# One attention-plus-MLP decode step on one core: the second and third pair's keys in one load each, their gathers moved to ScalarE and GpSimd

## The chip, the core and the metric

The kernel runs on one core of one Trainium2 chip. A core has five engines with an instruction queue each: PE (TensorE, matmuls), DVE (VectorE), ACT (ScalarE), POOL (GpSimd) and SP (SyncE, which here only issues DMAs). Sixteen DMA engines move data between HBM and the on-chip memory (SBUF). The metric is the device time of one execution in microseconds. Before the change its median over three runs is 189.87 us (189.81 to 189.93).

## What is computed

One new token (a row of 512 numbers) goes through grouped-query attention over a cache of 16384 positions and then through a small MLP:

```
q = layernorm(x) @ wq                          # 32 query heads of 128, 8 key/value heads
p = softmax(q . k_cache / sqrt(128))           # four query heads share one key head
h = x + (p . v_cache) @ wo
out = h + B(layernorm(h))                      # B: layernorm, w1 and w2 (one position: what they give is shifted
                                               #    out and padded with zeros), then gelu(layernorm(.) @ w3) @ w4
```

The caches have 8 heads of 16384 x 128 bf16 each, 4 MiB a head: 32 MiB of keys and 32 MiB of values. With wq, wo, w3 and w4 the core reads 79.17 MB in one execution, and each byte is used once. Position shifts in B leave nothing of w1 and w2 for a sequence of one position, so the kernel does not read them.

## The kernel before

**Pairs and halves.** The eight key heads are taken as four pairs. A pair's keys are 8 MiB: 128 partitions with 64 KB each (256 positions of 128 numbers). Its values have the same form. `kb_all` holds one pair's keys, seen as two halves `kb[0]` and `kb[1]` of 32 KB a partition; `vb` holds one pair's values; `kt` (32 KB a partition) holds half a pair's keys transposed. The first 4 MiB to arrive in `vb` are wq, and at the end wo goes into `kb[0]`, w3 and w4 into `kb[1]`.

**One pair** (the loop over `j` at the end of the function) goes like this:

1. DVE copies the pair's queries into `qn` (L704). For each half `y`, DVE transposes the keys from `kb[y]` to `kt` in 32x32 blocks of 4-byte elements (L616). A half has eight pieces. In pairs 0 to 2 an instruction takes two pieces, in the last pair mostly one.
2. PE clears a score bank (L627) and, piece by piece, multiplies queries and keys: four matmuls a piece, 32 a half (L633). DVE's transposes of the second half overwrite `kt` piece by piece as PE finishes the first half's.
3. `softmax` (L643 to L659): DVE's maximum, a small matmul that spreads it, ACT's exponential, and DVE's transposes of the result into `pt`. PE meanwhile runs 14 passes of two "unread" products (L498): matmuls whose result nobody reads, set in by `P.spin(14)` ahead of the matmul that sums the softmax (L678).
4. `values` (L670): 64 matmuls of `pt` with `vb` into the bank `O`.
5. `gather` (L687 to L696): DVE adds the four 128-column blocks of `O` with a mask weight each into `od` (one instruction, then three that continue it), PE multiplies `od` with `zo` (L694), and DVE scales the result into the pair's 32 rows of `o_m`. All on DVE and PE, so the next pair's `qn` copy and transposes stand behind it in DVE's queue.

**Who waits for what.** `Program` records every operation with what it reads and writes, and sets semaphore waits from that. Each engine runs its list in order. PE's part of the four pairs is not written out four times: `_tensor` emits one pair as a loop whose waits compare DVE's semaphore with a register that grows from piece to piece and from pair to pair. A wait for landed values goes through POOL: a no-op there waits for the DMA and then signals PE.

**Loads.** All large loads stand in SP's list and so in one order: wq, keys 0, values 0, keys 1 (two halves), values 1, keys 2 (two halves), values 2, keys 3 (two halves), values 3, wo (two parts), w3, w4 (three parts). Keys 0 are one load of 64 KB rows (L463 is the line of all loads, as a helper issues them). Half `y` of the next pair's keys is issued when DVE has transposed half `y` of this pair's; the next values when PE has read this pair's. An issued load stands behind the unfinished ones in the same queue.

**The end.** After the last pair DVE sums `o_m` (L732) and casts it (L734), PE runs 6 passes of unread products and multiplies with wo (L739), then follow layernorm (L743 to L531, ACT's L753), w3 (L759), gelu (L769), w4 (L782 and L794) and the 1 KB result's store.

Of the kernel before, what the change touches and what calls it, by code (L numbers as in the profile page):

```python
# [7 lines left out]
BF16 = mybir.dt.bfloat16  # L8
# [16 lines left out]
class Program:  # L25
# [150 lines left out]
    def _tensor(self):  # L176
# [51 lines left out]
        for o in loop:  # L228
            ds = [d for d in o.deps if d.own]
            assert not ds or o.at[0] == "value"  # L230
            assert not any(d.dma for d in o.deps)
            for d in ds:
                told.setdefault(o.at[1:3], set()).add((d.sem, d.val - d.worth + 1, d.val))
# [4 lines left out]
        assert v0 > 0 and first - step * last > 0  # L238

        r, rl, ry, rq, rk = (eng.alloc_register(n) for n in ("seen", "landed", "half", "query", "piece"))  # L240
        self.turn, self.turned = rk, KP * pieces
# [68 lines left out]
        def straight(kind):  # L310
            nonlocal now
            for a in places(kind, 1):
                self._spin(eng, at[a])
                v = rest.get((kind, a[-1]))
                if v is not None:
                    eng.reg_add(r, r, v - now)
                    eng.wait_ge(vector, r)
                    now = v
                self._issue(eng, at[a])
# [30 lines left out]
DH = 128  # L350
# [14 lines left out]
KP = 8 * DH  # L365
# [5 lines left out]
def bass_sequential_preLN__gqa_block_cached__mixer_s_mlp__decode_kernel(  # L371
# [13 lines left out]
    with ExitStack() as ctx:  # L385
# [60 lines left out]
        kb_all = sb("kb", [128, 256 * DH], BF16)  # L446
# [21 lines left out]
        def load_keys(j, y):  # L468
            n = 128 * DH
            load(f"k{y}", kb[y][:, :], pair_rows(A_k_cache, j)[:, y * n:(y + 1) * n], ("r", y, 0),  # L470
                 also=[("r", y, i) for i in range(1, RPARTS)])
# [55 lines left out]
        def variance(i):  # L527
# [7 lines left out]
            for n in range(1 + i):  # L535
# [9 lines left out]
        load("k", kb_all[:, :], pair_rows(A_k_cache, 0), ("r", 0, 0),  # L545
             also=[("r", y, i) for y in range(2) for i in range(RPARTS) if y or i])
# [65 lines left out]
        def transpose_keys(y, cuts):  # L612
            for t, n in zip(cuts, [b - a for a, b in zip(cuts, [*cuts[1:], 8])]):
                view = lambda x, t=t, n=n: x[:, :].bitcast(I32).rearrange("p (x l w) -> p x (l w)", x=2, l=64)[
                    :, :, t * 512:(t + n) * 512]
                P.op("DVE", lambda e, view=view: e.transpose(view(kt), view(kb[y])),  # L616
                     r=[("r", y, i) for i in range(RPARTS)], w=[("kt", t + i) for i in range(n)], worth=n)

        def key_piece(at, n):
            part = kt[:, :].rearrange("p (x f) -> p x f", x=2)[:, :, bass.ds(at, KP)]  # L620
            return part.rearrange("p x (l b s e) -> p b e x l s", l=8, b=2, s=32, e=2)[:, n // 2, n % 2, :, :, :]
# [40 lines left out]
        def values(j):  # L662
            tiles = vb[:, :].rearrange("p (x c l d) -> p x l c d", x=4, c=8, l=8)
            for x in range(VP):
                P.part("value", j, x)
                for it in range(16 // VP):
                    for ct in range(4):
# [4 lines left out]
                            tiles[:, l // 8, l % 8, 4 * ch:4 * ch + 4, :], start=(l < 2), stop=(l >= 30)),  # L672
# [8 lines left out]
        def gather(j):  # L681

            O, key = O_ps[0], ("O", 0)
            for c in range(4):
# [151 lines left out]
```

## Time and profile before

| | |
|---|---|
| median of three runs | 189.87 us |
| the profiled execution's own time | 189.89 us |
| its span, first to last instruction | 188.4 us |
| time outside the span | 1.49 us |
| busy: PE, DVE, ACT, POOL | 73%, 61%, 5%, 3% of the span |
| bytes read from HBM | 79.17 MB |
| mean granted TensorE clock | 0.898 of full |

The prediction reads four views. The page gives sums and the DMA engines' load. The timeline gives, for runs of like instructions, start, duration and in square brackets how long the engine had stood idle before and what ended that. The view of groups by shape gives the mean duration of one instruction of a kind. The view of windows cuts the span into stretches and gives PE's busy time, the granted TensorE clock (PEclk, 1.00 is full, 0.50 half), the share of DMA engines busy and the bandwidth in each; a transfer counts there with all its bytes where it starts, so in short windows the share can pass 1.

### The profile page before, as it was taken

Reading aid. Unit: us, or ns where it says so; the run is one execution under the profiler, and the core shown is the slowest. Engines: PE = TensorE matmul, PEld = TensorE weight load, DVE = VectorE, ACT = ScalarE, POOL = GpSimd, SP = SyncE. Lnnn points to the kernel's source line nnn. Section 1 sums busy time; section 2 is a strip of 40 time slices with the busy share of each in tenths; the row PEclk is TensorE's granted clock in tenths of the full one; section 3 lists DMA queues with packets and bytes.
Section 4 is the critical chain, followed back from the end, with each engine's and each line's share of the span. In section 5 each row is a group of like instructions: output and inputs, shape, how many; then the busy total and the mean of one; then the engine's idle time right before and its main releaser. Section 6 shows DMA issues by size and latency. Waiting matters only on the chain.

```text
span 188.4 us, 2532 instructions
## 1 busy us (share of the span) xinstructions
PE 137.8 (73%) x820; PEld 59.3 (31%) x824; DVE 115.8 (61%) x141; ACT 9.3 (5%) x16; POOL 5.9 (3%) x11
## 2 busy tenths in 40 slices
PE   1009700599989639998990999999319999886874
PEld 1004200234434413443450344345103433432332
DVE  4900741999645299994508999551449897513154
ACT  3000000000020000000200000020000000500011
POOL 1900000000000000000000000000000000000010
PEclk9999985569999975999998599999955999999998
DMA  6999999999799998999999999997999998899994
GB/s 223 445 445 445 445 445 445 445 445 445 334 445 445 445 543 362 417 389 403 445 445 445 445 445 445 445 445 334 445 445 445 556 403 362 362 440 450 397 411 183
DMA packets 2605, 79.19 MB, mean 420 GB/s; under 512 B 298, under 2 KB 300, under 8 KB 812
## 3 DMA queue, kind: packets, MB, share of 16 engines
q1 hardware_dynamic: 2596, 79.17, 97.9%
q8 instruction: 1, 0.02, 0.0%
q10 hardware_dynamic: 8, 0.00, 0.0%
HBM read 79.17 MB, written 0.00 MB: 420 GB/s over the span
## 4 chain that ended last, share of the span: by engine, by line
DMA 45%; PE 36%; DVE 16%; issue 2%; ACT 0%; SPq 0%; DVEq 0%
DMA kb<-in_A_k_cache_dram 32%; PE banks L633 22%; DMA kb<-in_B_w_dram 13%; DVE kt L616 12%; PE banks L498 6%; PE banks L670 4%; DVE mx L643 1%; PE banks L627 1%; DVE od L690 1%; PE banks L647 1%; PE banks L759 1%; PE banks L694 0%; DVE od L687 0%; DVE osum L785 0%; PE banks L782 0%
## 5 line engine op out<-in xcount | busy, mean ns | idle before, releaser
L616 DVE STREAM_TRANSPOSE kt<-kb 128x2048 int32<-128x2048 int32 (+1 forms) x37 | 71.0, 1985 | 10.4 <-DMA kb<-in_A_k_cache_dram 10.4
L633 PE MATMUL banks<-kt,qn 128*128 x256 | 69.1, 426 | 0.1
L633 PEld LDWEIGHTS banks<-kt,qn 128*128 x256 | 26.8, 105 | 41.0 <-issue 21.5
L498 PE MATMUL banks<-xn 128*128 128x512 bf16 x126 | 28.6, 381 | 0.0
L627 PE MATMUL banks<-qn 128*128 128x512 bf16 x8 | 3.9, 490 | 23.9 <-DVE kt L616 23.9
L498 PEld LDWEIGHTS banks<-xn 128*128 128x128 bf16 x130 | 12.7, 99 | 15.8 <-issue 2.4
L593 PE MATMUL banks<-vb,xn 128*128 x32 | 8.5, 432 | 9.7 <-DVE xn L584 9.7
L670 PE MATMUL banks<-vb,pt 128*32 128x512 bf16 x256 | 14.7, 379 | 0.7 <-POOLq L475 0.7
L659 DVE STREAM_TRANSPOSE pt<-p_sb 64x1024 bf16<-64x1024 bf16 x8 | 9.9, 1239 | 5.4 <-ACT p_sb L655 5.3
L655 ACT ACTIVATE p_sb<-banks,bias 128x1024 bf16<-128x1024 f32 x4 | 4.5, 1114 | 155.4 <-DVE nmh L651 155.4
L670 PEld LDWEIGHTS banks<-vb,pt 128*32 128x32 bf16 x256 | 8.7, 97 | 4.7 <-POOLq L475 0.8
L687 DVE TENSOR_SCALAR od<-banks,rowc 128x128 f32<-128x128 f32 x4 | 1.4, 351 | 14.2 <-PE banks L670 14.2
L643 DVE TENSOR_REDUCE mx<-banks 128x1 f32<-128x1024 f32 x4 | 4.9, 1224 | 8.1 <-PE banks L633 8.1
L627 PEld LDWEIGHTS banks<-qn 128*128 128x128 bf16 x8 | 0.8, 100 | 25.8 <-issue 25.4
L600 DVE STREAM_TRANSPOSE qcol<-banks 64x1024 f32<-64x1024 f32 x4 | 4.8, 1226 | 6.6 <-PE banks L593 6.6
L593 PEld LDWEIGHTS banks<-vb,xn 128*128 128x128 bf16 x32 | 3.5, 108 | 14.3 <-issue 11.6
L539 POOL TENSOR_TENSOR st<-st,expo 128x1 f32<-128x1 f32 (+1 forms) x2 | 1.3, 630 | 175.4 <-DVE st L537 175.4
L506 PE MATMUL banks<-mean 128*128 128x512 f32 (+1 forms) x12 | 6.5, 622 | 0.0
L694 PE MATMUL banks<-od,zo 128*32 128x128 f32 x8 | 1.6, 285 | 6.5 <-DVE od L690 6.5
L680 DVE RECIPROCAL den<-banks 32x1 f32<-32x1 f32 x4 | 0.6, 155 | 7.8 <-PE banks L678 7.8
L690 DVE SCALAR_TENSOR_TENSOR od<-banks,rowc,od 128x128 f32<-128x128 f32 x12 | 4.2, 351 | 0.4
L647 PE MATMUL banks<-mxd,mean 128*128 128x128 f32 x8 | 2.0, 326 | 2.4 <-DVE mxd L644 2.4
(81 smaller groups left out, 49.5 us busy)
## 6 DMA issues: line engine op xcount, KB each, us to landing
kb<-in_A_k_cache_dram SPq DMA_DIRECT2D x6, 4096.0 KB, 24.9
vb<-in_A_wq_dram SPq DMA_DIRECT2D x1, 4096.0 KB, 12.3
kb<-in_A_wo_dram SPq DMA_DIRECT2D x1, 3584.0 KB, 28.5
kb<-in_B_w_dram SPq DMA_DIRECT2D x1, 1792.0 KB, 24.2
kb<-in_B_w_dram SPq DMA_DIRECT2D x1, 896.0 KB, 26.0
kb<-in_B_w_dram SPq DMA_DIRECT2D x1, 640.0 KB, 27.1
kb<-in_A_wo_dram SPq DMA_DIRECT2D x1, 512.0 KB, 29.4
kb<-in_B_w_dram SPq DMA_DIRECT2D x1, 256.0 KB, 27.2
```

The source lines that it names most:

```text
L498: P.unread = lambda e: e.matmul(banks[:, 7, :], copies(xn[:, 0:1], 128), copies(xn[:, 0:1], 512), start=True, stop=True)
L506: pe(lambda e: e.matmul(banks[:, 7, 0:n], mean4[:, :], copies(mean4[:, 0:1], n), start=True, stop=True), r=["mean4"], w=["spare1"])
L593: pe(lambda e, k=k: e.matmul(row[:, bass.ds(P.b, 512)], copies(xn[:, k:k + 1], 128), wq_k[:, k, bass.ds(P.c, REP * DH)], start=(k == 0), s ...
L600: dve(lambda e, g=g, b=b, half=half: e.transpose(qcol[64 * g:64 * g + 64, 2 * b:2 * b + 2, :, :].rearrange("p e m u -> p (e m u)"), half.r ...
L616: P.op("DVE", lambda e, view=view: e.transpose(view(kt), view(kb[y])), r=[("r", y, i) for i in range(RPARTS)], w=[("kt", t + i) for i in r ...
L627: pe(lambda e: e.matmul(row[:, bass.ds(P.y, 512)], copies(none, 128), copies(none, 512), start=True, stop=False, skip_group_check=True), r ...
L633: pe(lambda e, n=n: e.matmul(row[:, bass.ds(P.y, 512)], qn[:, n, bass.ds(P.q, 128)], key_piece(P.k, n), start=False, stop=(n == 3), skip_g ...
L643: dve(lambda e: e.tensor_reduce(mx[:, :], s_all, AX.X, ALU.max), r=[("s", 0), ("s", 1)], w=["mx"], **both)
L655: act(lambda e: e.activation(p_sb[:, :], s_all, ACTF.Exp, bias=bias[:, 0:1], scale=float(SCALE), accum_out=acc[:, :]), r=[("s", 0), ("s", ...
L659: dve(lambda e, g=g: e.transpose(pt[64 * g:64 * g + 64, :, :, g, :], p_sb[64 * g:64 * g + 64, :]), r=["p"], w=["pt"])
L670: pe(lambda e, l=l, ct=ct, ch=ch: e.matmul(O_ps[0][32 * ct:32 * ct + 32, :], pt[:, l, ch, :, :].rearrange("p g u -> p (g u)"), tiles[:, l ...
L690: dve(lambda e, block=block, c=c: e.scalar_tensor_tensor(od[:, :], block, rowc[:, c:c + 1], od[:, :], ALU.mult, ALU.add), r=[key, "rowc", ...
```

## The change

- **Keys of pairs 1 and 2 in one load each.** They become one load of 64 KB rows, as keys 0 are already. Keys 3 stay two halves, because wo and w3/w4 are placed by halves after them. Instead of being issued in halves, such a load is issued when the transposes of *both* halves of the pair before are done, with one exception, the next point.
- **8 KB of shift a pair.** `kb_all` grows by 16 KB a partition. Keys 0 lie 16 KB into it, keys 1 8 KB, keys 2 and 3 at its start. So the next pair's keys do not overwrite the last 8 KB of this pair's, which are the last two pieces of the second half: the load does not wait for their transposes (the key `("tail", j)`).
- **Pieces.** A piece is now 16 neighbouring positions of a partition in one run (`KP` doubles) instead of 8 positions from each of two places; the sizes of all instructions stay. The second half is transposed piece by piece, eight instructions, in every pair. The indexing of `values` follows.
- **Three gathers on ScalarE and GpSimd.** In pairs 0 to 2 ACT scales the four blocks of `O` into `osum` (four activations), POOL adds them in two steps into `od`, PE waits for POOL; the result is scaled by ACT and masked by POOL into `o_m`. The last pair keeps the DVE form, and a no-op on POOL stands between DVE's `od` and PE.
- **Unread products growing by pair.** The passes ahead of L678 become a loop whose count is derived from the register of DVE's semaphore: 5, 8, 11 and 14 passes for pairs 0 to 3 in place of 14 each.

The core of the diff:

```diff
+                passes, body = self.spins.get(id(at[a]), (0, 0))
+                if passes:
+                    by = step // 3
+                    eng.reg_mov(self.turn, now - by * passes)
+                    eng.br("pe_turn")
+                    nc.switch_bb("pe_turn", parent=None)
+                    for _ in range(body):
+                        self.unread(eng)
+                    eng.reg_add(self.turn, self.turn, by)
+                    eng.br_lt(self.turn, r, "pe_turn", "pe_turned")
...
+                if any(d.own == "g" for d in at[a].deps):
+                    eng.wait_ge(self.gathered, rl)
...
-KP = 8 * DH
+KP = 16 * DH
+BASE = (4 * KP, 2 * KP, 0, 0)
...
-        kb_all = sb("kb", [128, 256 * DH], BF16)
+        kb_all = sb("kb", [128, BASE[0] + 256 * DH], BF16)
...
+            if y is None:
+                load("k", kb_all[:, BASE[j]:BASE[j] + 2 * n], pair_rows(A_k_cache, j), ("r", 0, 0),
+                     also=[("r", y, i) for y in range(2) for i in range(RPARTS) if y or i] + [("tail", j)])
...
+                at = BASE[j] + (8 * y + t) * KP
+                apart = BASE[j] and y and t >= 6
+                P.op("DVE", lambda e, t=t, n=n, at=at: e.transpose(
+                    kt[:, t * KP:(t + n) * KP].bitcast(I32), kb_all[:, at:at + n * KP].bitcast(I32)),
+                     r=[("tail", j)] if apart else [("r", y, i) for i in range(RPARTS)],
+                     w=[("kt", t + i) for i in range(n)], worth=n)
...
+            if j < PAIRS - 1:
+                for c in range(4):
+                    act(lambda e, c=c: e.activation(osum[:, c * 128:(c + 1) * 128], O[:, c * 128:(c + 1) * 128],
+                                                    ACTF.Identity, scale=rowc[:, c:c + 1]),
+                        r=[key, "rowc"], w=[("osum", c)], bank=[key])
+                pool(lambda e: e.tensor_tensor(osum[:, 0:256], osum[:, 0:256], osum[:, 256:512], ALU.add),
+                     r=[("osum", c) for c in range(4)] + [("o_m", j - 1)], w=[("osum", 0), ("osum", 1)])
+                P.op("POOL", lambda e: e.tensor_tensor(od[:, :], osum[:, 0:128], osum[:, 128:256], ALU.add),
+                     r=[("osum", 0), ("osum", 1)], w=["od", "gathered"], own="g")
+            else:
...
+                P.op("POOL", lambda e: e.nop(), r=["od"], w=["gathered"], own="g")
...
-                transpose_keys(y, (0, 2, 4, 6) if j < PAIRS - 1 else range(8) if y else (0, 1, 2, 4, 6))
+                transpose_keys(j, y, range(8) if y else (0, 2, 4, 6) if j < PAIRS - 1 else (0, 1, 2, 4, 6))
                 scores(j, y)
-                if j < PAIRS - 1:
+                if j == PAIRS - 2:
                     load_keys(j + 1, y)
+                elif j < PAIRS - 2 and y:
+                    load_keys(j + 1)
```

79 lines of the change are left out of this document (45 added, 34 removed).

## The prediction

> **What bounds the kernel now.** I read the page first: it says how full the DMA engines are.
>
> ```profile
> span 188.4 us, 2532 instructions
> ...
> PE 137.8 (73%) x820; PEld 59.3 (31%) x824; DVE 115.8 (61%) x141; ACT 9.3 (5%) x16; POOL 5.9 (3%) x11
> ...
> DMA  6999999999799998999999999997999998899994
> ...
> q1 hardware_dynamic: 2596, 79.17, 97.9%
> HBM read 79.17 MB, written 0.00 MB: 420 GB/s over the span
> ```
>
> SP's queue (q1) keeps the sixteen engines at 97.9% of the span. The DMA row gives their busy tenths in 40 slices: the first and the last slice are low, hardly any between. PE at 73% and DVE at 61% are the next busiest. That alone could hide small gaps, so I then took from the timeline the instructions that started because a load had landed.
>
> ```profile
> 13.14 0.29 DVE L584 TENSOR_SCALAR xn<-hT,st 128x4 bf16<-128x4 f32 x1 [3.54 <-DMA vb<-in_A_wq_dram]
> ...
> 32.47 17.66 DVE L616 STREAM_TRANSPOSE kt<-kb 128x2048 int32<-128x2048 int32 x8 [6.46 <-DMA kb<-in_A_k_cache_dram]
> ...
> 139.04 8.95 DVE L616 STREAM_TRANSPOSE kt<-kb 128x1024 int32<-128x1024 int32 x5 [3.17 <-DMA kb<-in_A_k_cache_dram]
> ...
> 148.74 9.13 DVE L616 STREAM_TRANSPOSE kt<-kb 128x1024 int32<-128x1024 int32 x8 [0.75 <-DMA kb<-in_A_k_cache_dram]
> ...
> 168.16 3.64 PE L670 MATMUL banks<-vb,pt 128*32 128x512 bf16 x64 [0.67 <-POOLq L475]
> ...
> 176.71 1.91 PE L739 MATMUL banks<-kb,o_b 128*32 128x512 bf16 x32 [0.17 <-DMA kb<-in_A_wo_dram]
> ...
> 182.29 0.94 PE L759 MATMUL banks<-kb,hc 128*32 128x448 bf16 x16 [0.34 <-DMA kb<-in_B_w_dram]
> ```
>
> These are the landings, in the queue's order, of wq, keys 0, the two halves of keys 3, values 3 (through POOL's no-op), wo and w3. Keys 0 (8 MiB) took 32.47 - 13.14 = 19.33 us. From there to the first half of keys 3 lie 44 MiB (values 0 to 2, keys 1 and 2, half of keys 3): 106.57 us, or 19.38 us for each 8 MiB. The next 4 MiB took 9.70 us (19.40 for 8), values 3 then 19.42. **One pace, 19.33 to 19.42 us for 8 MiB, from the second load to the last cache load:** the queue never ran dry, and no compute instruction between 13 and 168 us sets the end. After w3's landing a fixed chain of 6.1 us leads to the span's end (188.4 - 182.29).
>
> How far ahead of the queue is SP?
>
> ```profile
> 41.44 9.05 SPq L463 DMA_DIRECT2D kb<-in_A_k_cache_dram  x2
> 64.38 0.33 SPq L463 DMA_DIRECT2D vb<-in_A_v_cache_dram  x1
> 75.78 9.10 SPq L463 DMA_DIRECT2D kb<-in_A_k_cache_dram  x2
> ...
> 133.21 0.33 SPq L463 DMA_DIRECT2D vb<-in_A_v_cache_dram  x1
> ...
> 157.94 1.81 SPq L463 DMA_DIRECT2D kb<-in_B_w_dram  x4
> ```
>
> At 19.38 us a load, values 0 land at 32.47 + 19.38 = 51.85, keys 1 at 71.2, values 1 at 90.6, keys 2 at 110.0, values 2 at 129.3. Keys 1 were issued 10.4 us before values 0 landed (41.44), values 1 6.8 us before keys 1 landed (64.38), keys 2 14.8 us ahead (75.78), values 3 15.5 us ahead of the second half of keys 3 (133.21), w3 18.8 us before values 3 and wo were both in. So the kernel is bound by its bytes, and an edit can only count in four ways: the price of a load in the queue, a load issued too late, the chain before w3, the chain after it.
>
> **The change, part by part.**
>
> *Loads.* Two loads fewer, same bytes, same order. Two 4 MiB loads cost 2 x 9.70 = 19.40 us; whole 8 MiB loads cost 19.33 to 19.42. A merged pair thus gives -0.07 to +0.02 us, two of them -0.14 to +0.04. I take the middle, **-0.05 us**.
>
> The Trainium skill, page "DMA: Bandwidth & Descriptors", section "Anatomy of one DMA — SWDGE (gpsimd) path", speaks strongly for such a merge: it fits a DMA's time as about 2.0 us plus bytes at 436 GB/s. By that rule two loads fewer would save about 4.0 us (an estimate from that page). The trace does not agree for loads that stand behind others: 2.0 us more for each half would make 11.6 us, and the measured half took 9.70.
>
> *When the merged loads are issued.* This is what could cost something. In pair 0 the transposes start at 32.47 as before. The four instructions of the first half are done at 41.44, when SP issues. The second half is now eight instructions, as in the last pair: 9.13 / 8 = 1.14 us each. The load of keys 1 needs the first six: 41.44 + 6 x 1.14 = **48.3**. How long does an issue need until bytes flow?
>
> ```profile
> 0.74 0.40 SPq L463 DMA_DIRECT2D vb<-in_A_wq_dram  x1
> ```
> ```profile
> 1.60:1.80 0.20, 0.00 (x0) 0.00 (x0) 0.00 (x0) 0.20 (x1) 0.20 (x2) 1.00 2.06 494
> ```
>
> On the idle queue at the start: 1.60 - 0.74, about 1 us (the window row's last columns are DMA share and GB/s; the window before it moved nothing). From above: wq landed 12.40 us after its issue, where 4 MiB at the pace take 9.69, so at most 2.7 us with every start-up loss. Keys 1 must flow when values 0 end at 51.85: the issue may come between 49.1 (by 2.7) and 50.8 (by 1.0). At 48.3 it is in time by 0.8 to 2.5 us; I take the nearer row, 1.0 us, and so no gap. Keys 1 then land at 71.2 in one piece, and pair 1's transposes can only start there, as pair 0's did at their landing, while now the first half is at hand when DVE leaves pair 0's gather. Keys 2 are issued at 71.2 + 15.8 = 87.0 against 90.6: the same lead of 3.6 us. Pair 2 starts at 110.0. The shift is what carries this: if the load waited for all eight pieces, it would come at 50.6, in time by the one bound and 1.5 us late by the other.
>
> *Do the pieces of the second half come in time?* They overwrite `kt` behind PE.
>
> ```profile
> 44.89 0.38 PE L627 MATMUL banks<-qn 128*128 128x512 bf16 x1
> 45.10 7.29 PE L633 MATMUL banks<-kt,qn 128*128 x32
> ...
> 52.43 1.22 DVE L643 TENSOR_REDUCE mx<-banks 128x1 f32<-128x1024 f32 x1 [2.29 <-PE banks L633]
> ...
> 54.36 6.29 PE L498 MATMUL banks<-xn 128*128 128x512 bf16 x28
> ...
> 56.40 2.49 DVE L659 STREAM_TRANSPOSE pt<-p_sb 64x1024 bf16<-64x1024 bf16 x2 [1.34 <-ACT p_sb L655]
> ...
> 60.66 3.61 PE L670 MATMUL banks<-vb,pt 128*32 128x512 bf16 x61
> ...
> 65.90 0.41 PE L694 MATMUL banks<-od,zo 128*32 128x128 f32 x2 [1.63 <-DVE od L690]
> ```
>
> PE is done with the first half at 44.9; the sixth piece starts at 47.1. No wait. PE's own end of the second half (52.4) is bound by PE, 7.3 us after 45.1, so the maximum comes as before.
>
> *Fewer unread products.* `pt` is ready at 58.9, 26.4 us after a pair's start, whatever PE passes its time with; 28 products (0.22 us each) last until 60.6. With 10 and 16 products values start at 59.0 and end at 62.6, with 22 at 30.5 us after the start. That brings values 1 to 62.6 (needed by 71.2 - 2.7), values 2 to about 101.3 (needed by 107.3) and values 3 to 140.5 (needed by 146). In time: 0 us.
>
> *The three gathers.* They leave DVE (1.6 us a pair between values and L694) and move to ACT and POOL, and PE waits for those.
>
> ```profile
> L769 ACT ACTIVATE hg<-banks,st 128x224 bf16<-128x224 f32 x2 | 0.8, 488 | 1.7 <-PE banks L759 1.7
> L539 POOL TENSOR_TENSOR st<-st,expo 128x2 f32<-128x2 f32 x1 | 0.7, 702 | 172.2 <-DVE st L537 172.2
> L566 POOL COPY swapped<-ident_f 128x128 f32<-128x128 f32 x1 | 0.3, 290 | 0.0
> L799 ACT ACTIVATE fin<-banks 64x128 bf16<-64x128 f32 x1 | 0.3, 270 | 2.8 <-PE banks L794 2.8
> ```
>
> No row shows these operations. Four activations: 4 x 0.27 to 4 x 0.49; two additions: 2 x 0.29 to 2 x 0.70; hand-overs some 0.2: 1.9 to 3.6 us, and I take 2.6. Behind L694 in PE's queue stands the next pair's first half. In pairs 0 and 1 PE is done by 67 and 106, and the keys land at 71.2 and 110.0: hidden. In pair 2 it is not: keys 3's first pieces are ready at 140.4, and PE comes at 140.5 + 1.9 to 3.6 + 0.7 = 143.1 to 144.8.
>
> ```profile
> 140.42 0.60 PE L627 MATMUL banks<-qn 128*128 128x512 bf16 x1 [5.29 <-DVE kt L616]
> ...
> 150.54 0.38 PE L627 MATMUL banks<-qn 128*128 128x512 bf16 x1
> ...
> 159.12 1.22 DVE L643 TENSOR_REDUCE mx<-banks 128x1 f32<-128x1024 f32 x1 [1.25 <-PE banks L633]
> ```
>
> But today's first half took 10.1 us, cold; warm it is 7.3 (the 32 matmuls above), so it ends at 150.4 to 152.1, and the second ends at 157.7 to 159.4, where DVE's last piece (148.74 + 9.13 = 157.87) allows 159.0. So at most 0.4 us late. The cover: PE waited 0.67 us for values 3, then 0.17 for wo, then 0.34 for w3, **1.18 us in all**. The last pair's no-op on POOL (0 to 0.7 us by the POOL rows; a no-op computes nothing, I take 0.1) spends from the 0.51 behind values 3. Cost 0; without the cover up to 0.4 + 0.7 us.
>
> **Sum**: 189.89 (the profiled execution) - 0.05 = 189.84; it stands 0.02 above the median, so **189.8 us**. Own range 189.6 to 190.1.
>
> **Rivals.**
>
> *PE goes cold in pair 2's gather (slower).* The place is PE's wait for POOL. Windows of 3.41 us, cut so that clock changes fall on borders (third column from the right is the clock):
>
> ```profile
> 132.79:136.20 3.41, 0.71 (x10) 1.00 1.08 461
> 136.20:139.61 3.41, 0.00 (x0) 0.50 0.89 384
> ...
> 170.33:173.75 3.42, 1.80 (x31) 1.00 1.01 436
> ```
>
> With 0.71 us of work in it, a window was followed by half clock; with 1.80 it was not. A wait of 2.6 us leaves 0.8 if it falls into one window. Then the first half takes 10.1 instead of 7.3 us: from 143.1 to 144.8 on, the second half ends at 160.5 to 162.2, 1.4 to 3.1 us late, and after the cover of 1.18 the time grows by 0.2 to 1.9: 190.0 to 191.7, by the middle of each bound 190.7. It decides from a second half ending after 160.3. Against it: where windows start is chance, and some of the wait's places leave over 1.8 us. Chance 0.12.
>
> The Trainium skill, page "TensorE: Matmul & The Clock Gate", section "Part 1: The HAM clock gate", lets the clock fall only after an idle window of about 3.4 us, by which this rival would cost nothing; the first row above, 21% busy, differs, and decides.
>
> *A merged load comes late (slower).* Lead 0.8 to 2.5 us; whatever lengthens the six transposes beyond it, or the exception not holding in the program, costs its full length twice: up to 1.5 us each, 190.4 to 192.8. For it: these are the leads that shrink most, from 10.4 and 14.8 to 3.6 us. Against: DVE waits for nobody there. Chance 0.10.
>
> *The stream runs at its best pace (faster).* Eight cache loads at 19.33 instead of 19.40 save 0.5 us: 189.3; with a full price per load, at the utmost 185.9. For it: fewer issues; against: whole and split loads show one pace. Chance 0.08.
>
> **Chances and range.** Forecast 0.70, cold PE 0.12, late load 0.10, best pace 0.08. A measurement tells about 0.2% (0.38 us) from no change: faster 0.08, same 0.70, slower 0.22. 189.5 to 190.7 takes in the forecast, the milder half of the cold case (0.06) and the edges of the others (some 0.06), and leaves out the rest.
>
> **What would show it.** Right: landings of keys 3 near 139.0 and 148.7, w3 at 182.3; pair 1's and 2's transposes from 71.2 and 110.0; keys 1 issued near 48.3. Wrong: keys 1 or 2 landing later than that (late load), half clock after 143 with L643 after 160.3 (cold PE), or less than 19.3 us between landings of 8 MiB (best pace).

## The result and the profile after

The changed kernel takes **190.72 us** (median of 22 runs, 190.09 to 192.97) where the kernel before takes 189.89 us on the same chip (189.68 to 190.17, 22 runs): a ratio of 1.0048, 95% interval 1.0034 to 1.0062 (ratio and interval leave out the one execution counted as slow, 192.97 us). It is slower by half a per cent. The prediction was 189.8 us with no measurable change as the likeliest case; 190.72 lies 0.02 us above its range.

The profiled execution took 190.81 us. Its page:

```profile
span 189.5 us, 2446 instructions
...
PE 130.8 (69%) x788; PEld 54.4 (29%) x788; DVE 111.6 (59%) x138; ACT 13.8 (7%) x31; POOL 10.6 (6%) x20
...
DMA  6999999999999999999999999999999999989992
...
q1 hardware_dynamic: 2308, 79.17, 97.4%
```

By this page the queue is as full as before (97.4% against 97.9%), and no slice shows a hole. So the loss is not to be found in shares; the times of the landings show it. In the timeline of the changed kernel, DVE's transposes of the four pairs start when the keys land:

```profile
32.63 17.90 DVE L639 STREAM_TRANSPOSE kt<-kb 128x2048 int32<-128x2048 int32 x12 [5.07 <-DMA kb<-in_A_k_cache_dram]
...
72.08 17.90 DVE L639 STREAM_TRANSPOSE kt<-kb 128x2048 int32<-128x2048 int32 x12 [12.23 <-DMA kb<-in_A_k_cache_dram]
...
110.75 17.90 DVE L639 STREAM_TRANSPOSE kt<-kb 128x2048 int32<-128x2048 int32 x12 [11.46 <-DMA kb<-in_A_k_cache_dram]
...
139.75 8.95 DVE L639 STREAM_TRANSPOSE kt<-kb 128x1024 int32<-128x1024 int32 x5 [1.46 <-DMA kb<-in_A_k_cache_dram]
...
149.46 9.13 DVE L639 STREAM_TRANSPOSE kt<-kb 128x1024 int32<-128x1024 int32 x8 [0.76 <-DMA kb<-in_A_k_cache_dram]
```

Subtract neighbours. From keys 1 to keys 2 lie 16 MiB: 110.75 - 72.08 = 38.67 us, or 19.34 for 8 MiB, the old pace. To the first half of keys 3 (12 MiB) 29.00, to the second 9.71: the old pace again. Only the first stretch, keys 0 to keys 1, is long: 72.08 - 32.63 = **39.45 us** for 16 MiB. About 0.75 us is lost once, between 32 and 72 us, and all later landings carry it: keys 3 come at 139.75 and 149.46 where they came at 139.04 and 148.74.

What happened in that stretch? SP's part of the timeline and, behind it, the view of DMA issues for the stretch from 48 to 60 us:

```profile
23.99 0.33 SPq L483 DMA_DIRECT2D vb<-in_A_v_cache_dram  x1
48.35 0.33 SPq L483 DMA_DIRECT2D kb<-in_A_k_cache_dram  x1
62.90 0.33 SPq L483 DMA_DIRECT2D vb<-in_A_v_cache_dram  x1
87.80 0.33 SPq L483 DMA_DIRECT2D kb<-in_A_k_cache_dram  x1
```
```profile
kb<-in_A_k_cache_dram SPq DMA_DIRECT2D x1, 23.6
```

Keys 1 are issued at 48.35, as predicted (48.3), and land 23.6 us later. The trace also holds the single transfers of each DMA engine, rows of 64 KB. They follow each other on every engine, and a row takes 2.42 us, in all kernels here. The engines finished values 0 between 50.67 and 51.73. Fourteen of the sixteen took up keys 1 at once and one within 0.1 us; the last, as far as the times tell engines apart, was done at 51.45 and began at 51.85, a gap of 0.40 us. And the sixteen first rows of keys 1 took 2.77 us in the mean and up to 3.26. So did, less so, the last row of values 0 on the slowest engine (2.61) and some second rows of keys 1 (up to 2.62); then rows took 2.42 again. From keys 0 to keys 1 the sixteen engines lost 0.44 us in the mean, 0.03 of it idle, and the last one 0.76. A load has landed when its last engine is done; here that was the engine with the gap, whose first row took 2.87 us.

The second difference is on PE, in the last pair:

```profile
143.81 0.41 PE L730 MATMUL banks<-od,zo 128*32 128x128 f32 x2 [2.27 <-POOL od L716]
144.37 0.39 PE L652 MATMUL banks<-qn 128*128 128x512 bf16 x1 [0.16 <-DVE kt L639]
144.70 8.25 PE L658 MATMUL banks<-kt,qn 128*128 x32
153.16 0.39 PE L652 MATMUL banks<-qn 128*128 128x512 bf16 x1 [0.20 <-DVE kt L639]
153.49 8.27 PE L658 MATMUL banks<-kt,qn 128*128 x32
...
163.72 6.29 PE L522 MATMUL banks<-xn 128*128 128x512 bf16 x28
...
170.02 3.61 PE L695 MATMUL banks<-vb,pt 128*32 128x512 bf16 x61
...
178.40 1.91 PE L785 MATMUL banks<-kb,o_b 128*32 128x512 bf16 x32
...
183.57 0.94 PE L805 MATMUL banks<-kb,hc 128*32 128x448 bf16 x16
```

The last three rows carry no bracket: PE no longer waits for values 3, wo or w3, as it did before (0.67, 0.17 and 0.34 us). Here PE sets the end, and the loads are in ahead of it.

So there are two suspects: the slow start of keys 1, which delays every landing by some 0.7 us, and PE's lateness in the last pair. The experiments take them apart. Each is compared with the kernel before in runs on the same chip (189.79 to 189.90 us there).

### The profile page after: what moved, and what is told of

Its sections match the earlier page's. It is cut to its first block, busy times and chain, and to the rows that moved or that the text cites. A ratio compares the mean times of both kernels' runs of the same rounds, so it can differ in the third digit from the quotient of the medians.

```text
span 189.5 us, 2446 instructions
## 1 busy us (share of the span) xinstructions
PE 130.8 (69%) x788; PEld 54.4 (29%) x788; DVE 111.6 (59%) x138; ACT 13.8 (7%) x31; POOL 10.6 (6%) x20
## 3 DMA queue, kind: packets, MB, share of 16 engines
q1 hardware_dynamic: 2308, 79.17, 97.4%
## 4 chain that ended last, share of the span: by engine, by line
DMA 52%; DVE 31%; PE 15%; issue 1%; ACT 0%; SPq 0%; DVEq 0%; POOLq 0%
DMA kb<-in_A_k_cache_dram 52%; DVE kt L639 28%; PE banks L522 5%; PE banks L658 4%; PE banks L695 2%; PE banks L785 1%; DVE mx L668 1%; DVE od L725 1%; PE banks L530 1%; PE banks L805 0%; DVE osum L831 0%; DVE osum L789 0%; PE banks L828 0%; DVE hcol L819 0%; ACT hg L815 0%
## 5 line engine op out<-in xcount | busy, mean ns | idle before, releaser
L639 DVE STREAM_TRANSPOSE kt<-kb 128x1024 int32<-128x1024 int32 (+1 forms) x49 | 71.8, 1533 | 31.0 <-DMA kb<-in_A_k_cache_dram 31.0
L658 PE MATMUL banks<-kt,qn 128*128 x256 | 67.2, 408 | 0.1
L658 PEld LDWEIGHTS banks<-kt,qn 128*128 x256 | 25.9, 101 | 39.8 <-issue 21.8
L522 PE MATMUL banks<-xn 128*128 128x512 bf16 x94 | 22.2, 381 | 0.0
L616 PE MATMUL banks<-vb,xn 128*128 x32 | 9.9, 485 | 9.6 <-DVE xn L607 9.6
L522 PEld LDWEIGHTS banks<-xn 128*128 128x128 bf16 x94 | 9.1, 99 | 11.5 <-issue 2.6
L695 PEld LDWEIGHTS banks<-vb,pt 128*32 128x32 bf16 x256 | 8.2, 97 | 4.5
L714 POOL TENSOR_TENSOR osum<-osum 128x256 f32<-128x256 f32 x3 | 2.2, 723 | 127.2 <-ACT osum L711 127.2
L616 PEld LDWEIGHTS banks<-vb,xn 128*128 128x128 bf16 x32 | 3.8, 120 | 15.2 <-issue 13.3
L730 PE MATMUL banks<-od,zo 128*32 128x128 f32 x8 | 1.7, 290 | 8.2 <-POOL od L716 6.8
L711 ACT ACTIVATE osum<-banks,rowc 128x128 f32<-128x128 f32 x12 | 3.4, 368 | 19.4 <-PE banks L695 19.4
L604 DVE COPY zo<-rowgh 128x32 f32<-128x32 f32 x1 | 3.6, 3633 | 0.0
```

The source lines that it names most:

```text
L522: P.unread = lambda e: e.matmul(banks[:, 7, :], copies(xn[:, 0:1], 128), copies(xn[:, 0:1], 512), start=True, stop=True)
L604: dve(lambda e, z=z, m=m: e.tensor_copy(z[:, :].rearrange("p (n d) -> p n d", d=4), m[:, :, :].rearrange("p g h -> p (g h)").unsqueeze(2). ...
L616: pe(lambda e, k=k: e.matmul(row[:, bass.ds(P.b, 512)], copies(xn[:, k:k + 1], 128), wq_k[:, k, bass.ds(P.c, REP * DH)], start=(k == 0), s ...
L639: P.op("DVE", lambda e, t=t, n=n, at=at: e.transpose(kt[:, t * KP:(t + n) * KP].bitcast(I32), kb_all[:, at:at + n * KP].bitcast(I32)), r=[ ...
L658: pe(lambda e, n=n: e.matmul(row[:, bass.ds(P.y, 512)], qn[:, n, bass.ds(P.q, 128)], key_piece(P.k, n), start=False, stop=(n == 3), skip_g ...
L695: pe(lambda e, l=l, ct=ct, ch=ch: e.matmul(O_ps[0][32 * ct:32 * ct + 32, :], pt[:, l, ch, :, :].rearrange("p g u -> p (g u)"), tiles[:, l ...
```

## The experiments

**Fewer products for PE, loads as changed** (4, 6, 8 and 10 passes instead of 5, 8, 11 and 14).

```diff
-                    by = step // 3
+                    by = 10
...
-            P.spin(14)
+            P.spin(10)
```

> The changed kernel with 4, 6, 8 and 10 passes of unread products instead of 5, 8, 11 and 14. Theory LATE PE: pair 2's gather on ScalarE and GpSimd holds PE until 144.4 us, pair 3's two halves then take 8.6 us each on a warm PE (1.03 us a piece), its maximum starts 2.7 us late (161.8 instead of 159.1), and values 3 no longer wait for their load. Four passes fewer in the last pair give back 8 x 0.22 = 1.75 us, so values start near 168.9 at the landing of values 3 and the time falls to that of the kernel before within 0.3 us: 189.8 to 190.2. Theory LATE LOAD: keys 1, issued with only 2.4 us of values 0 left, lose 0.4 to 0.8 us on their first rows and everything behind them lands as much later; the passes change nothing, 190.6 to 190.8.

Measured 190.57 us, ratio 1.004 (1.0026 to 1.0055). PE waits again:

```profile
168.90 3.64 PE L695 MATMUL banks<-vb,pt 128*32 128x512 bf16 x64 [0.69 <-POOLq L499]
...
183.04 0.94 PE L805 MATMUL banks<-kb,hc 128*32 128x448 bf16 x16 [0.36 <-DMA kb<-in_B_w_dram]
```

Values 3 and w3 now end PE's waits, at times 0.74 and 0.75 us later than before (168.16, 182.29). Keys 1 were issued at 48.35 again, and their first rows took 2.79 us in the mean. So PE's lateness is not the main loss.

**Keys 1 and 2 in halves again, all else as changed.**

```diff
-BASE = (4 * KP, 2 * KP, 0, 0)
+BASE = (0, 0, 0, 0)
...
-                if j == PAIRS - 2:
+                if j < PAIRS - 1:
                     load_keys(j + 1, y)
-                elif j < PAIRS - 2 and y:
-                    load_keys(j + 1)
```

> The changed kernel with keys 1 and 2 again in two halves each, at the places and with the issue times of the kernel before; pieces, gathers on ScalarE and GpSimd and passes as changed. Both theories blame the merged loads, by different ways. LATE PE: pairs 1 and 2 start when their first half has landed (61.5 and about 100.5), pair 2 is done by about 132, PE waits for keys 3 as before: 189.8 to 190.0, and the maximum of pair 3 at 159.1. LATE LOAD: the first rows of keys 1 take no longer than others, same 189.8 to 190.0. A rival to both, that the gathers themselves cost (ScalarE and GpSimd disturb the transfers), expects 190.5 or more here.

Measured 189.71 us, ratio 0.9998 (0.9989 to 1.0008). The loss is gone. The moved gathers, the pieces and the grown loop of products cost nothing by themselves; the merged loads do.

**The merged loads alone.** The kernel before, with merged loads, shift and pieces as changed; the gathers stay on DVE and every pair has 14 passes.

```diff
-KP = 8 * DH
+KP = 16 * DH
+BASE = (4 * KP, 2 * KP, 0, 0)
...
-        kb_all = sb("kb", [128, 256 * DH], BF16)
+        kb_all = sb("kb", [128, BASE[0] + 256 * DH], BF16)
...
-                if j < PAIRS - 1:
+                if j == PAIRS - 2:
                     load_keys(j + 1, y)
+                elif j < PAIRS - 2 and y:
+                    load_keys(j + 1)
```

> The kernel before with the merged loads, the shift and the new pieces alone: gathers stay on DVE, 14 passes in every pair. LATE PE: pair 2 starts at 110.0 to 110.7, its values end near 142.2 (28 products), DVE's gather ends at 144.5, only then do the transposes of pair 3's first half start (5 us later than 139.0), its second half's end at 144.5 + 18.1 = 162.6, the maximum starts near 164, that is 5 us late, less 1.2 us of cover: 193 to 194.5, slower than the whole change. LATE LOAD: the same loss as the whole change, 190.6 to 190.8.

Measured 194.2 us, ratio 1.0227 (1.0207 to 1.0248). DVE's timeline shows why:

```profile
143.05 1.12 DVE L696 SCALAR_TENSOR_TENSOR od<-banks,rowc,od 128x128 f32<-128x128 f32 x3
...
145.28 17.96 DVE L620 STREAM_TRANSPOSE kt<-kb 128x1024 int32<-128x1024 int32 x13
```

The first transposes of keys 3 have no bracket: they did not wait for the load but for DVE's own gather of pair 2, and start at 145.28 instead of 139.75. A merged load delays its pair by half a load, and DVE's gather then stands ahead of keys 3. The changed kernel, with the gathers off DVE and fewer products in pairs 0 to 2, loses 3.5 us less; how much of that each of the two brings was not tried apart.

**No shift: the merged loads wait for all eight pieces.**

```diff
-                apart = BASE[j] and y and t >= 6
+                apart = False
```

> The changed kernel with the exception taken away: the loads of keys 1 and 2 wait for all eight pieces of the second half and are issued 2.3 us later (near 50.6 and 90.1 instead of 48.35 and 87.8). The first engine runs out of values 0 at 50.7. LATE LOAD: 1 to 2 us more for keys 1 and as much again for keys 2, 192.5 to 194.5. LATE PE: the queue stands still for 0.5 to 1 us each time and everything behind it moves, landings and PE alike: 191.5 to 192.5. If an issue needs no lead at all: 190.7, as changed.

Measured 192.59 us, ratio 1.0144 (1.0129 to 1.016). Keys 1 are issued at 50.23, and the first row starts at 51.20, 0.97 us later: all sixteen engines had been done by 51.16 and stood idle. The first rows took 3.10 us in the mean. From keys 0 to keys 1 and on to keys 2 lie 39.81 and 40.16 us, against 38.7 without loss. A load that meets an idle engine pays the gap and slow first rows.

**Issue keys 1 earlier.** The shift between pairs 0 and 1 grows to 16 KB (the tile `qcol` lies in `kt` to make room), so that keys 1 wait for four pieces. Once with the fewer products of the first experiment, once with the changed kernel's own 5, 8, 11 and 14 passes.

```diff
-BASE = (4 * KP, 2 * KP, 0, 0)
+BASE = (6 * KP, 2 * KP, 0, 0)
...
-                apart = BASE[j] and y and t >= 6
+                apart = BASE[j] and y and t >= 8 - (BASE[j] - BASE[j + 1]) // KP
```

> e1_fewer_last (4, 6, 8, 10 passes) with 16 instead of 8 KB of shift between keys 0 and keys 1, so that the load of keys 1 needs only the first four pieces of the second half; it is issued 2.3 us earlier, near 46.1. The queries' transposed form lies in the tile of the transposed keys, free at that time, to make room. LATE LOAD: the first rows of keys 1 take 2.42 us again as all others, not up to 3.6, keys 1 land near 71.1 instead of 71.6, the engine that lags falls away and the time goes from 190.57 to 189.7 to 189.9. If the slow first rows come from something else at 50.6 to 51.6 us (the place in memory that is written, or work beside it) and not from the issue: 190.5 as in e1.

> The changed kernel with its own 5, 8, 11 and 14 passes and the early load of e5. It has left only PE's lateness in pair 3. LATE LOAD alone: 189.7 to 189.9, as e5. LATE PE: keys 2 land at 110.0, the maximum of pair 3 starts near 161.0 (1.9 us after 159.1; the gather of pair 2 ends at 143.1), less 1.2 us of cover: 190.3 to 190.6.

Measured 189.78 us (0.9993, 0.9984 to 1.0002) and 190.00 us (1.0006, 0.9997 to 1.0015). Keys 1, issued at 45.8, have first rows of 2.42 and 2.45 us. With the slow start gone, what is left of the loss is the difference of the two: **0.22 us for PE's lateness** (two other pairs of kernels here that differ in the passes alone give 0.15 and 0.29). The slow start's share, the same passes with the load early or not, is 0.7 to 0.9 us.

**Keys 1 in halves, keys 2 merged** (with the fewer products):

```diff
-BASE = (4 * KP, 2 * KP, 0, 0)
+BASE = (2 * KP, 2 * KP, 0, 0)
...
-                if j == PAIRS - 2:
+                if j != 1 and j < PAIRS - 1:
                     load_keys(j + 1, y)
-                elif j < PAIRS - 2 and y:
+                elif j == 1 and y:
                     load_keys(j + 1)
```

> e1_fewer_last with keys 1 in two halves, issued near 41.3 and 50.5 as in the kernel before, and only keys 2 in one load (issued early, near 78, since pair 1 then starts at its first half's landing). LATE LOAD: no load is late, 189.7 to 189.9, though pair 2 starts at 110 as in the change. A theory that 64 KB rows of keys are slower in themselves, or that pair 2's late start costs by itself: 190.2 or more.

Measured 189.65 us, ratio 0.9988 (0.9979 to 0.9997), a little faster than the kernel before. Keys 2 in one load cost nothing.

**Issue keys 1 later.** They wait for seven pieces instead of six (with the fewer products):

```diff
-                apart = BASE[j] and y and t >= 6
+                apart = BASE[j] and y and t >= (7, 6)[j]
```

> e1_fewer_last with the load of keys 1 one piece later: it waits for seven pieces of the second half and is issued near 49.5, 1.1 us before the first engine ends values 0 at 50.6. LATE LOAD: the loss grows as the lead shrinks, between e1 (lead 2.3 us, 190.57) and e4's 1.4 us a load: 190.9 to 191.4, with all first rows of keys 1 near 3 us. If the lead does not matter as long as there is some: 190.5 to 190.6 as e1.

Measured 189.77 us, ratio 0.9996 (0.9987 to 1.0005): the theory that the load lost its lead falls. Keys 1 were issued 0.8 us *later* than in the changed kernel and landed earlier, 21.8 us behind their issue, as the same view of DMA issues says for this kernel:

```profile
kb<-in_A_k_cache_dram SPq DMA_DIRECT2D x1, 21.8
```

First rows: 2.47 us in the mean, 2.70 at most. The landings of keys 0, keys 1 and keys 2 lie 38.70 and 38.71 us apart:

```profile
32.30 17.90 DVE L639 STREAM_TRANSPOSE kt<-kb 128x2048 int32<-128x2048 int32 x12 [5.38 <-DMA kb<-in_A_k_cache_dram]
...
71.00 17.90 DVE L639 STREAM_TRANSPOSE kt<-kb 128x2048 int32<-128x2048 int32 x12 [11.48 <-DMA kb<-in_A_k_cache_dram]
...
109.71 17.90 DVE L639 STREAM_TRANSPOSE kt<-kb 128x2048 int32<-128x2048 int32 x12 [11.51 <-DMA kb<-in_A_k_cache_dram]
```

**The same edit on the changed kernel with its own passes.**

```diff
-                apart = BASE[j] and y and t >= 6
+                apart = BASE[j] and y and t >= (7, 6)[j]
```

> The changed kernel with its own 5, 8, 11 and 14 passes of unread products; the one edit is that keys 1 wait for one transpose more, so that they are issued at 49.15 us instead of 48.35. SLOW ROWS (keys 1, issued at 48.35, get first rows of 64 KB that take up to 0.8 us longer than the 2.42 us of all others, and everything behind them lands late): they are gone here as they were in e8_later, and only TensorE's lateness is left, so the time is that of e6_early_14 against before, 1.0006: 190.0 us, range 189.8 to 190.2. LATE TENSORE (the 8.6 us of a half of pair 3 behind the gather makes the whole loss, and the slow rows none): 190.6 to 190.8, as the changed kernel. LEAD (a load issued later is filled later): 191 or more.

Measured 190.06 us, ratio 1.0008 (0.9997 to 1.0018). Moving one issue by about a microsecond takes away most of the loss. In the profiled execution, which at 190.51 us was the slowest of its eleven, the first rows still took 2.73 us: a late issue is mostly, not always, clean.

**A small delay through GpSimd, which went astray** (with the fewer products):

```diff
+                if j == 0 and y and t + n == 6:
+                    pool(lambda e: e.memset(od[:, :], 0.0), r=[("kt", 5)], w=["od", "pad"])
```

> e1_fewer_last (4, 6, 8 and 10 passes), with one GpSimd memset of a 128x128 tile behind the sixth transpose that keys 1 wait for: issued some 0.3 to 0.5 us later than the 48.35 us, between e1_fewer_last (190.57 us, 1.0041) and e8_later (issued 49.15, 189.77, 0.9996). BAD MOMENT, wide (the stretch in which an issue slows the rows reaches from 2.3 us ahead of the end of the load ahead to the 2.7 us above): first rows mean 2.4 to 2.5 us and 189.8. BAD MOMENT on both sides: still slow, 190.5. LEAD alone would make it slower than e1_fewer_last; it fell with e8_later and is kept for completeness.

Measured 192.83 us, ratio 1.0164 (1.015 to 1.0178). It did not test what it was meant to: keys 1 were issued at 52.27 instead of about 48.7. POOL's queue already held the no-op that waits for values 0, and the memset stood behind it:

```profile
51.98 0.20 POOL L644 MEMSET od<- 128x128 f32 x1 [42.30 <-DMA vb<-in_A_v_cache_dram]
```

It shows once more what an empty queue costs: 41.76 us from keys 0 to keys 1.

**The changed kernel once more**, unchanged, for a second trace.

> The changed kernel once more, letter for letter, for a second trace of it. SLOW ROWS belong to the program (its moment of issue): the first rows of keys 1 take a mean of 2.8 us again, and the time is 190.7. SLOW ROWS belong to the one execution or to the chip: first rows of 2.42 us and, in the profiled execution, a last landing as early as before, with a time that differs from 190.7 by over 0.3 us.

Measured 190.85 us, ratio 1.0053 (1.0038 to 1.0069). Keys 1 were issued at 48.00, their first rows took 2.94 us in the mean and 3.64 at most, and keys 1 came 39.98 us after keys 0. Six engines stood idle before them, which makes 0.25 us in the mean of all sixteen; one began keys 1 only at 52.19, 4.19 us after the issue. The slow start belongs to the program.

**Keys 1 after five pieces** (a shift of 12 KB, with the fewer products):

```diff
-BASE = (6 * KP, 2 * KP, 0, 0)
+BASE = (5 * KP, 2 * KP, 0, 0)
```

> e5_early with a shift of 12 KB in place of 16 KB between pairs 0 and 1: keys 1 wait for five pieces and are issued near 47.5 us, between e5_early (45.83, 189.78) and e1_fewer_last (48.35, 190.57). BAD MOMENT (an issue about 2.3 us ahead of the end of the load ahead, and no other): 189.8. If the stretch reaches up to 3.1 us ahead: 190.3 to 190.6, with first rows of keys 1 of over 2.6 us.

Measured 189.65 us, ratio 0.9991 (0.9982 to 1.0). Issued at 46.91, first rows of 2.42 us.

**Small delays through ScalarE.** One activation after the sixth piece on the loads of the first experiment; two after the fifth piece, on the kernel just shown; and two after the sixth piece of pair 1, ahead of keys 2, on that kernel too.

```diff
+                if j == 0 and y and t + n == 6:
+                    for i in range(1):
+                        act(lambda e, i=i: e.activation(od[:, 64 * i:64 * i + 64], ident_f[:, 0:64],
+                                                        ACTF.Identity, scale=rowc[:, 0:1]),
+                            r=[("kt", t), "ident_f", "rowc"], w=[("od", i), "pad"])
```

The load of keys 1 (or 2) writes the key `"pad"` too, here and in the GpSimd experiment, and so waits for the added work.

> e1_fewer_last with one ScalarE activation of 128x64 behind the sixth transpose that keys 1 wait for as well: issued near 48.75 us, between e1_fewer_last (48.35, 190.57 us) and e8_later (49.15, 189.77). LEAD ABOUT ONE ROW (the bad leads are those near the 2.42 us that a row takes, and 1.9 us as for keys 2 are good): first rows of 2.4 to 2.5 us and 189.8. KEYS 1 ALONE (the moment is bad for keys 1 from 48.0 to somewhere below 49.15, whatever keys 2 do): open, 189.8 or 190.5.

> e12_mid_early with two ScalarE activations of 128x64 behind the fifth transpose that keys 1 wait for as well: issued near 47.5 us, a lead of 3.2 us, between e12_mid_early (46.91, 189.65) and the changed kernel's second trace (48.00, 190.85). LEAD ABOUT ONE ROW: 189.7. A wider bad stretch: 190.3 to 190.6.

> e12_mid_early with two ScalarE activations of 128x64 behind the sixth transpose of pair 1 that keys 2 wait for as well: keys 2 issued near 87.3 us, a lead of 2.2 us, which lies inside the leads that slowed keys 1 (2.3 in the changed kernel) or just beside them. LEAD ABOUT ONE ROW: keys 2 get slow first rows, and the time rises to 190.3 to 190.6. KEYS 1 ALONE: no slow rows, 189.7.

Measured 190.68 us (1.0053, 1.0029 to 1.0076), 189.66 us (0.9989, 0.9979 to 0.9999) and 189.58 us (0.9984, 0.9974 to 0.9994). Keys 1 issued at 48.77 are slow (first rows 2.82 us in the mean, 4.16 at most), issued at 47.46 they are not. Keys 2, moved to 87.49, show nothing.

The profiled execution of the first of the three took 193.09 us and shows a second loss that follows from the first:

```profile
32.65 17.90 DVE L639 STREAM_TRANSPOSE kt<-kb 128x2048 int32<-128x2048 int32 x12 [6.49 <-DMA kb<-in_A_k_cache_dram]
...
73.17 17.90 DVE L639 STREAM_TRANSPOSE kt<-kb 128x2048 int32<-128x2048 int32 x12 [13.30 <-DMA kb<-in_A_k_cache_dram]
...
112.82 17.90 DVE L639 STREAM_TRANSPOSE kt<-kb 128x2048 int32<-128x2048 int32 x12 [12.44 <-DMA kb<-in_A_k_cache_dram]
```

There the slowest engine ended keys 1 2.30 us behind the first. DVE starts pair 1 by the slowest engine, 40.52 us after pair 0; so keys 2 are issued late, at 88.89, only 0.90 us before the fastest engine has ended values 1 (89.79). That engine runs dry for 0.3 us, twelve of the sixteen stand idle, keys 2's first rows take 2.97 us in the mean, and the next stretch too is long: 39.65 us. Two of the changed kernel's 22 executions took 192.9 us; that they are of this kind is likely, but neither was profiled.

All traces with keys 1 in one load, by the moment of issue counted from the start of pair 0's transposes, as executions differ by some tenths there. "Idle" is what the sixteen engines stood still in the mean between their last row of values 0 and their first of keys 1:

| keys 1 issued | after pair 0's start | kernel | keys 0 to keys 1, us | idle, mean us | first rows, mean us |
|---|---|---|---|---|---|
| 45.82 | 13.48 | sixteen KB of shift, changed passes | 38.77 | 0.00 | 2.45 |
| 45.83 | 13.48 | sixteen KB of shift, fewer products | 38.71 | 0.00 | 2.42 |
| 46.91 | 14.60 | five pieces | 38.70 | 0.00 | 2.42 |
| 47.04 | 14.60 | five pieces, two activations in pair 1 | 38.69 | 0.00 | 2.42 |
| 47.46 | 15.23 | five pieces and two activations | 38.71 | 0.00 | 2.42 |
| 48.35 | 15.72 | changed kernel | 39.45 | 0.03 | 2.77 |
| 48.00 | 15.72 | changed kernel, second trace | 39.98 | 0.25 | 2.94 |
| 48.33 | 15.72 | merged loads alone | 39.56 | 0.06 | 2.72 |
| 48.35 | 15.73 | fewer products | 39.47 | 0.02 | 2.79 |
| 48.77 | 16.12 | fewer products and one activation | 40.52 | 0.00 | 2.82 |
| 49.15 | 16.85 | seven pieces, fewer products | 38.70 | 0.00 | 2.47 |
| 49.48 | 16.85 | seven pieces, changed passes | 38.90 | 0.03 | 2.73 |
| 50.23 | 17.97 | all pieces | 39.81 | 0.42 | 3.10 |
| 52.27 | 19.74 | fewer products and the memset | 41.76 | 2.52 | 3.02 |

There is a bad moment for keys 1: all five traces with an issue 15.7 to 16.1 us after pair 0's start lose 0.75 us or more between keys 0 and keys 1, none of the five up to 15.2 loses 0.1, and at 16.85, before the queue runs dry, one trace is nearly clean and the other loses 0.2 us. Most of the loss is slow rows; idle engines add to it in some traces. What makes the moment bad is **not settled**. It is not the lead alone: in the changed kernel's second trace keys 1 were issued 2.68 us before the first engine ended values 0 and were slow, in the kernel with five pieces keys 2 were issued 2.70 us before that of values 1 (86.73, 89.43), with first rows of 2.43. (One trace stands between: with 16 KB of shift and the changed passes keys 2 were issued 2.73 us ahead, and their first rows took 2.58.) Nor is it the place in memory: with six pieces and with seven, keys 1 are written to the same place. Nor is it the place in DVE's work: keys 2 of the changed kernel are issued at 87.80, 15.72 us after pair 1's start, the very moment that is bad for keys 1, with first rows of 2.42. No other transfer runs in the trace at 50 to 55 us.

## Why the prediction was wrong, point by point

- **The pace and the bound: right.** Outside the one stretch the changed kernel's queue delivers 8 MiB in 19.33 to 19.42 us, from keys 1 to the second half of keys 3. In the other kernels it takes 19.32 to 19.48 there, but for the two traces where keys 2 too were issued late (all pieces, and the 193.09 us execution).
- **Merging two loads saves 0.05 us: right in being nothing.** Keys 1 came 38.70 us after keys 0 when merged and on time (seven pieces), and 38.71 in two halves (71.17 - 32.46), as DVE's timeline of the kernel with keys 1 in halves says:

```profile
32.46 17.90 DVE L639 STREAM_TRANSPOSE kt<-kb 128x2048 int32<-128x2048 int32 x12 [5.12 <-DMA kb<-in_A_k_cache_dram]
61.53 8.89 DVE L639 STREAM_TRANSPOSE kt<-kb 128x2048 int32<-128x2048 int32 x4 [1.84 <-DMA kb<-in_A_k_cache_dram]
71.17 9.13 DVE L639 STREAM_TRANSPOSE kt<-kb 128x1024 int32<-128x1024 int32 x8 [0.75 <-DMA kb<-in_A_k_cache_dram]
```

 The Trainium skill, page "DMA: Bandwidth & Descriptors", section "Anatomy of one DMA — SWDGE (gpsimd) path", gives a DMA that GpSimd issues about 2.0 us on top of its bytes. SP issues the loads here, and these two numbers show no such price for one that stands behind another.
- **"At 48.3 it is in time by 0.8 to 2.5 us; I take the nearer row, 1.0 us, and so no gap": this step failed.** The issue was at 48.35. The step counted the lead up to the landing of values 0 (51.85), which is the end of the last engine; the first was done at 50.67, so its lead was 2.3 us, below the step's own upper bound of 2.7. And it took "in time" to mean "without loss". In the changed kernel's two traces the engines stood idle for 0.03 and 0.25 us in the mean, and the first rows were slow by 0.35 and 0.52 us in the mean and by up to 0.84 and 1.22 on one engine; the slowest engine sets the landing. The prediction's rival of a late merged load had the right place and price, in its lower part. A lead that is too short, which it named, is not the whole cause: issued 0.8 us later, with seven pieces, keys 1 cost next to nothing.
- **The gathers take 1.9 to 3.6 us (2.6 taken): right.** In the last gather that ACT and POOL do,

```profile
141.27 1.14 ACT L711 ACTIVATE osum<-banks,rowc 128x128 f32<-128x128 f32 x4 [6.66 <-PE banks L695]
...
142.49 0.72 POOL L714 TENSOR_TENSOR osum<-osum 128x256 f32<-128x256 f32 x1 [36.35 <-ACT osum L711]
143.30 0.46 POOL L716 TENSOR_TENSOR od<-osum 128x128 f32<-128x128 f32 x1
```

 ACT began at 141.27 and PE's L730 at 143.81: 2.5 us. PE came to pair 3 at 144.37, less the 0.7 us by which all was late 143.7, inside 143.1 to 144.8. The no-op in the last pair (0.1 us taken) was right too: PE's product with `zo` begins 0.13 us behind DVE's `od`, before the change 0.06.
- **"warm it is 7.3": wrong in size.** The halves run from 144.37 to 153.16 and from there to the maximum,

```profile
161.80 1.23 DVE L668 TENSOR_REDUCE mx<-banks 128x1 f32<-128x1024 f32 x1 [3.21 <-PE banks L658]
```

 8.8 and 8.6 us, at full clock. The prediction's own rows had such a half, 150.54 to 159.12 in the last pair before; it read that one as held up by DVE, which is so for the last piece alone (there the weights come at 158.03, behind DVE's end at 157.87). The maximum thus came 2.0 us later than its landings explain (161.80 - 159.12 - 0.7), where "at most 0.4 us late" stood. The weight loads show why. In the last pair of the changed kernel they come in fours, every 1.05 us, and ahead of each four the view names nothing but PE's own issue:

```profile
146.76 0.63 PEld L658 LDWEIGHTS banks<-kt,qn 128*128 x4 [0.44 <-issue]
147.82 0.56 PEld L658 LDWEIGHTS banks<-kt,qn 128*128 x4 [0.44 <-issue]
148.87 0.56 PEld L658 LDWEIGHTS banks<-kt,qn 128*128 x4 [0.49 <-issue]
```

 The 7.3 us came from pair 0 of the kernel before, where PE had the instructions in hand:

```profile
44.89 5.09 PEld L633 LDWEIGHTS banks<-kt,qn 128*128 x24
50.30 0.56 PEld L633 LDWEIGHTS banks<-kt,qn 128*128 x4 [0.32 <-issue]
51.35 0.56 PEld L633 LDWEIGHTS banks<-kt,qn 128*128 x4 [0.49 <-issue]
```

 Twenty-four loads without a break, then the same rhythm. Pair 0 had a stock of issued instructions (its clock had been at half until 40.6 us, so that issue could run ahead; this part is argued, not tried). The changed kernel's own pairs fit: the clock is half for the first 5.1, 3.2 and 5.5 us of pairs 0 to 2 and never in pair 3, and the 32 matmuls of their second halves take 7.55, 8.26, 7.36 and 8.27 us. A PE that comes to a pair late has none, and eight pieces cost some 8 x 1.04 us.
- **Fewer unread products cost 0 us: right for the three pairs that got fewer.** What it missed is the last pair, which kept 14 passes. With the maximum 2.0 us late, `pt` is ready at 165.75 + 2.49 = 168.24, as DVE's timeline says,

```profile
165.75 2.49 DVE L684 STREAM_TRANSPOSE pt<-p_sb 64x1024 bf16<-64x1024 bf16 x2 [1.33 <-ACT p_sb L680]
```

 while the 28 products last until 170.0. So the cover of 1.18 us did not reach: 0.22 us came through, and ten passes take it back.
- **Cold PE: did not decide.** In both traces of the changed kernel the clock is full from 119 us to the end. It can happen: in the 193.09 us execution (fewer products, one activation) this windows view has 0.99 us of work in one window and half clock (third column from the right) in the next.

```profile
143.14:146.56 3.42, 0.99 (x5) 0.29 (x4) 3.42 (x3) 1.40 (x5) 1.29 (x3) 1.00 1.03 441
146.56:149.98 3.42, 3.42 (x9) 1.26 (x10) 3.42 (x3) 0.00 (x0) 0.28 (x1) 0.50 1.32 565
```

 PE still waited 1.29 us for values 3 afterwards, so it cost nothing there. The Trainium skill, page "TensorE: Matmul & The Clock Gate", section "Part 1: The HAM clock gate", has the clock fall after an idle window; a window 29% busy was enough here.
- **The sum.** 0.75 us from the slow start of keys 1 and 0.22 from PE make 0.97; the medians differ by 0.83 to 0.95.

Better than both kernels are the versions that keep merged loads, issue keys 1 earlier and run 4, 6, 8 and 10 passes: 189.65 us with five pieces, 189.58 with keys 2 a little later as well, 0.1 to 0.2% under the kernel before. That is the most that two loads fewer are worth here; what the other changes bring was tried only with halves and 5 to 14 passes (189.71 us, no change).

## What to carry to other kernels

Where a DMA queue is the bound, compare landings load by load, not the queue's share: a loss of 0.75 us hid behind a full row of nines. Count a transfer's lead to the end of the first engine, not to the landing, which is the end of the last. A transfer issued in time to leave next to no gap can still start slowly, so measure one issue earlier and one later before the lead is called safe. And take a stage's duration from an instance in the state in which it will run: a half that starts with issued instructions in hand says little on one that starts late.

## What the runs showed of the hardware

- A load that meets busy engines can have slow first rows: 2.72 to 2.94 us in the mean for 64 KB instead of 2.42 in the five traces with the issue 15.7 to 16.1 us after pair 0's start; an issue at 15.2 was clean, at 16.85 one trace had 2.47 and one 2.73.
- Single engines can wait for a load issued 2.3 to 2.7 us before the first of them is done: one for 0.40 us in the changed kernel's first trace, six in its second, the last of which began 4.19 us after the issue.
- A load that meets engines already done began to flow 0.97 us after its issue (all pieces; its last engine 1.86), and its first rows took 3.1 us.
- On a PE that came late, at full clock, the score matmuls ran at some 1.04 us for four, with 0.44 to 0.49 us of issue ahead of each four weight loads.
- An operation on GpSimd waits behind a no-op there that waits for a transfer: the memset meant for 48.7 us ran at 51.98.
